# Six of 64 chunk stores issued by GpSimd in pieces of seven and eight rows

## The chip, the cores and the metric

The kernel runs on one core of a Trainium2 chip. The core has five engines that this text names: PE (TensorE, matrix products), DVE (VectorE), ACT (ScalarE), POOL (GpSimd) and SP (SyncE, which here issues loads only). Sixteen DMA engines move data between the chip's memory (HBM) and the core's on-chip memory SBUF, whose 128 rows are called partitions; PE writes into a second on-chip memory, PSUM. DMAs are issued by SP, ACT or GpSimd, each through a queue of its own. The metric is device time in microseconds (us) for one execution; lower is better.

## What is computed

The input is an image of 512 by 512 pixels with 192 channels, in bfloat16. The channels fall into four groups of 48, and each group is multiplied with its own 48 by 48 matrix (a grouped convolution with a window of one pixel):

```python
H = W = 512; G = 4; C = 192; Cg = 48; k = 1
x: (1, H, W, C) bfloat16        w: (1, 1, G, Cg, Cg) bfloat16

xg = x.reshape(1, H, W, G, Cg)
out = einsum('bhwgc,gcd->bhwgd', xg, w[0, 0])
return out.reshape(1, H, W, C)
```

So 262,144 pixels come in and go out, 384 B each: 100.66 MB in and as much out.

## The kernel before

**Tiling.** The pixels are cut into 64 chunks of 4096 pixels. A chunk is a tile of 128 partitions by 32 pixels, so that a partition's row is 32 x 384 = 12,288 B without a break in HBM, and a chunk is 1536 KB. rows_view (L102) gives a chunk's rows of the input or output. There are NB = 5 input buffers x_sb and 5 output buffers o_sb; chunk n uses buffer n mod 5 of each.

**Work on a chunk.** A chunk is eight groups of four pixels a partition. For each group PE makes six transposes (L192) of 128 by 128 from x_sb into PSUM (xT_ps); DVE copies the result to SBUF (L242, xT_sb); PE multiplies the six pieces with a prepared weight tile wt (L214, into o_ps in PSUM); and the result goes from o_ps to o_sb as bfloat16. That last step, the eviction, is ACT's (L285, both halves of a group), but in three groups of ten (SHARE, L34) ACT takes one half (L282) and DVE the other (L249). PE transposes two groups ahead of the products (LOOK).

**Order and waits.** Each engine runs its own list of instructions, and semaphores hold it back. The Waiter class (L37) leaves out a wait that an earlier one already covers.

- SP issues the load of chunk n (L160) once PE has transposed all of chunk n - 5.
- ACT issues the store of chunk n in its function store (L255 to L269), when it has come to the third group of the next chunk: the wait on mm_done (L263) is for the product two groups after the chunk's last, by which its evictions are known to be done.
- A store is one DMA of 128 rows. It adds 16 to the semaphore st_sem of its buffer, one for each DMA engine that has written its part. Before ACT writes the first group of chunk n into o_sb, it waits for the store of chunk n - 5 (L274); DVE does the same (L246). The amounts to wait for are counted by store_parts and st_total (L106 to L112).
- GpSimd makes two constants at the start (L140 to L151, the identity for the transposes and a selection tile for the weights) and does nothing afterwards.
- At the end ACT waits for all stores (L291).

The names RELIEF and RELIEF_ROWS (L28, L29) let chosen stores be issued in several ranges of rows; RELIEF is empty, so no store is split. The lines that issue a store:

```python
dst = rows_view(of, n)
for (r0, r1) in store_parts(n):
    act.dma_start(dst[r0:r1, :], o_sb[b][r0:r1, 0:sizes[n] * C]).then_inc(st_sem[b], 16)
```

Of the kernel before, what the change touches and what calls it, by code (L numbers as in the profile page):

```python
# [6 lines left out]
BF16 = mybir.dt.bfloat16  # L7
# [4 lines left out]
C = GROUPS * CG  # L12
# [12 lines left out]
PPC = 32  # L25
NB = 5
TAIL = (32, 32, 32, 32)
RELIEF = ()  # L28
RELIEF_ROWS = ((0, 128),)  # L29
NXP = 4  # L30
NOB = 4
NXS = 4
# [17 lines left out]
def shared(g):  # L50
    return (g % 10) in SHARE


def bass_standalone__grouped__vision_kernel(nc, x, w, out):
# [9 lines left out]
    sizes = [PPC] * n_mid + list(TAIL)  # L64
    n_chunks = len(sizes)

    xf = x.rearrange("b h w c -> (b h w) c")
    of = out.rearrange("b h w c -> (b h w) c")
# [12 lines left out]
    g1 = [g0[n] + sizes[n] // 4 for n in range(n_chunks)]  # L81
# [14 lines left out]
    def actT_cnt(g):  # L96
        return g - GT + 1

    def dveT_cnt(g):
        return sum(1 for h in range(GT, g + 1) if shared(h))  # L100

    def rows_view(ap, n):  # L102
        s = sizes[n]
        return ap[pix0[n]:pix0[n] + 128 * s, :].rearrange("(p i) c -> p (i c)", p=128)

    def store_parts(n):  # L106
        return RELIEF_ROWS if n in RELIEF else ((0, 128),)

    st_total, acc = [], [0] * NB
    for n in range(n_chunks):  # L110
        acc[n % NB] += 16 * len(store_parts(n))
        st_total.append(acc[n % NB])  # L112

    def st_before(n):
        return st_total[n - NB] if n >= NB else 0

    with ExitStack() as es:
        block = es.enter_context(nc.Block())
        x_sb = [es.enter_context(nc.sbuf_tensor(f"x_sb{i}", [128, PPC * C], BF16)) for i in range(NB)]
        o_sb = [es.enter_context(nc.sbuf_tensor(f"o_sb{i}", [128, PPC * C], BF16)) for i in range(NB)]  # L120
# [2 lines left out]
        esel = es.enter_context(nc.sbuf_tensor("esel", [CG, ECOLS], BF16))  # L123
        w_sb = es.enter_context(nc.sbuf_tensor("w_sb", [CG, GROUPS, CG], BF16))
        wt = es.enter_context(nc.sbuf_tensor("wt", [128, WCOLS], BF16))
        xT_ps = es.enter_context(nc.psum_tensor("xT_ps", [128, NXP, 1024], BF16))
        o_ps = es.enter_context(nc.psum_tensor("o_ps", [128, NOB, 512], F32))

        def sem(name):
            return es.enter_context(nc.semaphore(name))  # L130

        ld_sem = [sem(f"ld{i}") for i in range(NB)]
        st_sem = [sem(f"st{i}") for i in range(NB)]
        w_sem, id_sem, e_sem, wb_sem = sem("w_sem"), sem("id_sem"), sem("e_sem"), sem("wb_sem")
        p0_sem, p1_sem, wc_sem = sem("p0_sem"), sem("p1_sem"), sem("wc_sem")
        t_done, mm_done = sem("t_done"), sem("mm_done")
        ev1_sem, ev2_sem, act_sem = sem("ev1_sem"), sem("ev2_sem"), sem("act_sem")
        ev2T_sem, actT_sem = sem("ev2T_sem"), sem("actT_sem")

        @block.gpsimd  # L140
        def _(gp):
            gp.memset(esel[:], 1.0).then_inc(p0_sem, 1)  # L142
            gp.memset(ident[:], 1.0).then_inc(p1_sem, 1)  # L143
            gp.wait_ge(p0_sem, 1)
            gp.affine_select(out=esel[:], in_=esel[:], pattern=[[-1, ECOLS]],  # L145
                             compare_op=AluOpType.is_equal, fill=0.0, base=ESHIFT,
                             channel_multiplier=1).then_inc(e_sem, 1)
            gp.wait_ge(p1_sem, 1)
            gp.affine_select(out=ident[:], in_=ident[:], pattern=[[-1, 128]],  # L149
                             compare_op=AluOpType.is_equal, fill=0.0, base=0,  # L150
                             channel_multiplier=1).then_inc(id_sem, 1)  # L151

        @block.sync
        def _(sp):
# [77 lines left out]
        @block.vector  # L232
        def _(dve):
            wq = Waiter(dve)
            wq.wait(wb_sem, 1)
            dve.tensor_copy(wt[:], o_ps[:, NOB - 1, 0:WCOLS]).then_inc(wc_sem, 1)  # L236
            waited_chunk = -1
            for (op, g) in dve_prog:
                n, lg = groups[g]
                if op == "ev1":  # L240
                    wq.wait(t_done, g + 1)
                    dve.tensor_copy(xT_sb[g % NXS][:], xT_ps[:, g % NXP, 0:2 * UC]).then_inc(ev1_sem, 1)  # L242
                else:
                    if waited_chunk != n:
                        waited_chunk = n
                        wq.wait(st_sem[n % NB], st_before(n))  # L246
                    wq.wait(mm_done, g + 1)
                    u = lg * 2 + 1
                    dve.tensor_copy(o_sb[n % NB][:, u * UC:(u + 1) * UC],  # L249
                                    o_ps[:, (2 * g + 1) % NOB, 0:UC]).then_inc(  # L250
                                        ev2_sem if g < GT else ev2T_sem, 1)

        @block.scalar
        def _(act):
            wq = Waiter(act)  # L255
            act.sem_inc(act_sem, 2)
            pending = []

            def store(n):
                b = n % NB  # L260
                g = g1[n] - 1
                if g < GT:
                    wq.wait(mm_done, g + 3)  # L263
                else:
                    wq.wait(actT_sem, actT_cnt(g))
                    wq.wait(ev2T_sem, dveT_cnt(g))
                dst = rows_view(of, n)
                for (r0, r1) in store_parts(n):
                    act.dma_start(dst[r0:r1, :], o_sb[b][r0:r1, 0:sizes[n] * C]).then_inc(st_sem[b], 16)  # L269

            for g in range(NG):
                n, lg = groups[g]
                if lg == 0:
                    wq.wait(st_sem[n % NB], st_before(n))  # L274
                wq.wait(mm_done, g + 1)
                while pending and pending[0][1] <= g:
                    store(pending.pop(0)[0])
                v = (2 * g) % NOB
                ob = o_sb[n % NB]
                if shared(g):  # L280
                    u = lg * 2
                    ins = act.copy(ob[:, u * UC:(u + 1) * UC], o_ps[:, v, 0:UC])  # L282
                else:
                    dst = ob[:, lg * 2 * UC:(lg + 1) * 2 * UC].rearrange("p (u c) -> p u c", u=2)
                    ins = act.copy(dst, o_ps[:, v:v + 2, 0:UC])  # L285
                ins.then_inc(act_sem if g < GT else actT_sem, 1)
                if g == g1[n] - 1:
                    pending.append((n, g + 2 if g < GT else g + 1))
            for (n, _) in pending:
                store(n)  # L290
            for b in range(NB):  # L291
                act.wait_ge(st_sem[b], acc[b])
# [28 lines left out]
```

## Time and profile before

| | |
|---|---|
| device time, median of 3 runs | 494.31 us (494.1 to 494.51) |
| the profiled execution | 494.62 us, of which the span from the first to the last instruction is 492.9 us |
| granted clock of TensorE, mean over the span | 0.986 |
| busy, share of the span | PE 84%, DVE 71%, ACT 71%, POOL 0% |
| HBM read, written | 100.68 MB, 100.66 MB; 409 GB/s together, mean over the span |
| loads | 64 of 1536 KB on SP's queue (q1), median 30.9 us from issue to landing |
| stores | 64 of 1536 KB on ACT's queue (q10), median 30.5 us from issue to landing |

How to read the profile: the page cuts the span into 40 equal slices; each digit is the busy share of a slice in tenths, 9 standing for 90% and more. DMA is the mean busy share of the 16 DMA engines. The chain of waits follows the work that ended last back from the end: at each step to what released it. A group of instructions is given by line, engine, operation, written and read tile, count, busy time, mean duration of one, and the idle time before it. ACTq and SPq are the instructions by which an engine issues DMAs. "Issue to landing" is the time from that instruction to the last of the DMA's semaphore increments.

### The profile page before, as it was taken

Reading aid. Unit: us, or ns where it says so; the run is one execution under the profiler, and the core shown is the slowest. Engines: PE = TensorE matmul, PEld = TensorE weight load, DVE = VectorE, ACT = ScalarE, POOL = GpSimd, SP = SyncE. Lnnn points to the kernel's source line nnn. Section 1 sums busy time; section 2 is a strip of 40 time slices with the busy share of each in tenths; the row PEclk is TensorE's granted clock in tenths of the full one; section 3 lists DMA queues with packets and bytes.
Section 4 is the critical chain, followed back from the end, with each engine's and each line's share of the span. In section 5 each row is a group of like instructions: output and inputs, shape, how many; then the busy total and the mean of one; then the engine's idle time right before and its main releaser. Section 6 shows DMA issues by size and latency. Waiting matters only on the chain.

```text
span 492.9 us, 15013 instructions
## 1 busy us (share of the span) xinstructions
PE 415.4 (84%) x6154; PEld 390.5 (79%) x6154; DVE 348.0 (71%) x666; ACT 349.0 (71%) x513; POOL 1.3 (0%) x8
## 2 busy tenths in 40 slices
PE   4888999999999888888888888888888888888880
PEld 4788999999989887787777877878778787787770
DVE  2767888888888776776776767677667767777760
ACT  1757888888888767677677776766767667676680
POOL 1000000000000000000000000000000000000000
PEclk9989999999999999999999999999999999999995
DMA  8999999999999999999999999999999999999563
GB/s 342 398 428 426 427 429 427 428 428 428 429 428 429 430 429 430 429 430 428 427 430 430 429 429 429 430 428 427 429 428 430 428 427 430 430 430 430 213 266 144
DMA packets 18658, 201.56 MB, mean 409 GB/s; under 512 B 2256, under 2 KB 2256, under 8 KB 2256
## 3 DMA queue, kind: packets, MB, share of 16 engines
q1 hardware_dynamic: 9424, 100.69, 48.3%
q10 hardware_dynamic: 9216, 100.67, 48.2%
q8 instruction: 7, 0.11, 0.1%
q14 instruction: 11, 0.09, 0.0%
HBM read 100.68 MB, written 100.66 MB: 409 GB/s over the span
## 4 chain that ended last, share of the span: by engine, by line
DMA 67%; PE 2%; ACT 1%; ACTq 0%; issue 0%
DMA out_dram<-o_sb 67%; PE o_ps L214 1%; ACT o_sb L285 1%; PE xT_ps L192 1%; ACTq L269 0%; ACT o_sb L282 0%; ACTq L47 0%
## 5 line engine op out<-in xcount | busy, mean ns | idle before, releaser
L285 ACT CAST o_sb<-o_ps 128x768 bf16<-128x768 f32 x359 | 280.1, 799 | 99.9 <-PE o_ps L214 65.4
L242 DVE COPY xT_sb<-xT_ps 128x768 bf16<-128x768 bf16 x512 | 282.3, 554 | 89.4 <-PE xT_ps L192 84.3
L214 PE MATMUL o_ps<-wt,xT_sb 128*128 128x144 bf16 (+1 forms) x3072 | 297.5, 233 | 46.9 <-PEq L169 40.5
L192 PE MATMUL xT_ps<-ident,x_sb 128*128 128x128 bf16 x3072 | 256.7, 220 | 10.0 <-PEq L169 4.9
L214 PEld LDWEIGHTS o_ps<-wt,xT_sb 128*128 128x128 bf16 x3072 | 210.9, 98 | 64.4 <-issue 51.5
L192 PEld LDWEIGHTS xT_ps<-ident,x_sb 128*128 128x128 bf16 x3072 | 196.8, 98 | 17.2 <-issue 17.1
L249 DVE CAST o_sb<-o_ps 128x384 bf16<-128x384 f32 x153 | 84.6, 553 | 32.9 <-DMA out_dram<-o_sb 20.0
L282 ACT CAST o_sb<-o_ps 128x384 bf16<-128x384 f32 x153 | 73.4, 480 | 30.7 <-DMA out_dram<-o_sb 19.6
L178 PE MATMUL o_ps<-w_sb,esel 48*128 48x48 bf16 x10 | 0.6, 209 | 7.3 <-DMA w_sb<-in_w_dram 7.3
L236 DVE CAST wt<-o_ps 128x480 bf16<-128x480 f32 x1 | 0.7, 658 | 7.9 <-PE o_ps L178 7.9
L178 PEld LDWEIGHTS o_ps<-w_sb,esel 48*128 48x128 bf16 x10 | 0.5, 110 | 7.3 <-issue 7.3
L285 ACT ACT_TABLE_LOAD x1 | 1.3, 1283 | 0.9 <-PEq L306 0.9
L145 POOL TENSOR_SCALAR_AFFINE_SELECT esel<-esel 48x272 bf16<-48x272 bf16 x1 | 0.4, 406 | 0.0
L142 POOL MEMSET esel<- 48x272 bf16 x1 | 0.3, 318 | 0.3 <-POOLq L306 0.3
L149 POOL TENSOR_SCALAR_AFFINE_SELECT ident<-ident 128x128 bf16<-128x128 bf16 x1 | 0.3, 286 | 0.0
L143 POOL MEMSET ident<- 128x128 bf16 x1 | 0.2, 198 | 0.0
L306 POOL MEMSET const-bfloat16-1.0<- 128x1 bf16 x1 | 0.1, 102 | 0.0
L306 POOL MEMSET const-uint8-127<- 128x1 uint8 x1 | 0.1, 102 | 0.0
L306 POOL MEMSET const-float32-1.0<- 128x1 f32 x1 | 0.1, 99 | 0.0
L306 POOL MEMSET const-float32-0.0<- 128x1 f32 x1 | 0.1, 98 | 0.3 <-issue 0.3
## 6 DMA issues: line engine op xcount, KB each, us to landing
x_sb<-in_x_dram SPq DMA_DIRECT2D x64, 1536.0 KB, 30.9
out_dram<-o_sb ACTq DMA_DIRECT2D x64, 1536.0 KB, 30.5
w_sb<-in_w_dram SPq DMA_DIRECT2D x1, 18.0 KB, 5.9
```

Source lines behind the costliest of these rows:

```text
L142: gp.memset(esel[:], 1.0).then_inc(p0_sem, 1)
L145: gp.affine_select(out=esel[:], in_=esel[:], pattern=[[-1, ECOLS]], compare_op=AluOpType.is_equal, fill=0.0, base=ESHIFT, channel_multipli ...
L149: gp.affine_select(out=ident[:], in_=ident[:], pattern=[[-1, 128]], compare_op=AluOpType.is_equal, fill=0.0, base=0, channel_multiplier=1) ...
L178: last = pe.matmul(o_ps[:, NOB - 1, col:col + CG], lhsT=esel[:, s0:s0 + 128], rhs=w_sb[:, g, :], start=True, stop=True, skip_group_check=True)
L192: last = pe.transpose(xT_ps[:, g % NXP, j * 128:(j + 1) * 128], x_sb[b][:, col:col + 128], ident[:])
L214: last = pe.matmul(o_ps[:, v, c0:c1], lhsT=xs[:, j * 128:(j + 1) * 128], rhs=wt[:, WOFF[tc]:WOFF[tc] + (c1 - c0)], start=(tc == 0), stop=( ...
L236: dve.tensor_copy(wt[:], o_ps[:, NOB - 1, 0:WCOLS]).then_inc(wc_sem, 1)
L242: dve.tensor_copy(xT_sb[g % NXS][:], xT_ps[:, g % NXP, 0:2 * UC]).then_inc(ev1_sem, 1)
L249: dve.tensor_copy(o_sb[n % NB][:, u * UC:(u + 1) * UC], o_ps[:, (2 * g + 1) % NOB, 0:UC]).then_inc(ev2_sem if g < GT else ev2T_sem, 1)
L282: ins = act.copy(ob[:, u * UC:(u + 1) * UC], o_ps[:, v, 0:UC])
L285: ins = act.copy(dst, o_ps[:, v:v + 2, 0:UC])
L306: nc = _bacc.Bacc("TRN2", target_bir_lowering=False, num_devices=1)
```

## The change

Stores 5, 14, 23, 32, 41 and 50 (RELIEF) are no longer one DMA on ACT's queue. GpSimd issues them, in pieces, once the same product count is reached on which ACT's store waits.

- For each of eight values j a piece of seven rows is stored (rows r, r + 4, ... r + 24, where r runs over 0 to 3 and 32 to 35), then a "skip" follows, then a piece of eight rows (64 + r, ... in steps of four).
- A skip copies one element in each of so many partitions of a small new tile, scratch, to another column of it. It is a DMA like the others and stores nothing of the result..
- The pieces leave out rows 28 to 31 and 60 to 63 (QUADS). quad_home gives each such group of four one of three ways: ACT stores it as a DMA of four rows (act_parts), or GpSimd does, with a skip of 12 behind it, or with a skip of 4 ahead and one of 8 behind. Over the six stores each way is taken by four of the twelve groups.

In sum GpSimd issues 164 DMAs (104 of rows and 60 skips) and ACT 58 whole stores and four of four rows. ACT and DVE get one more wait each ahead of chunk n: for the pieces of chunk n - 5, on the new semaphores gs_sem. GpSimd waits for its own DMAs at the end. The other 58 stores, the loads and all computation are as before.

```diff
-RELIEF = ()
-RELIEF_ROWS = ((0, 128),)
+RELIEF = tuple(range(5, 55, 9))
+QUADS = (28, 60)
+
+
+def quad_home(n, q):
+    return (2 * RELIEF.index(n) + q) % 3
+
+
+def act_parts(n):
+    if n not in RELIEF:
+        return [(0, 128)]
+    return [(QUADS[q], 4) for q in range(2) if quad_home(n, q) == 0]
+
+
+def gp_parts(n):
+    parts = []
+    for j in range(8):
+        r = 32 * (j // 4) + j % 4
+        parts += [("rows", r, 4, 7), ("skip", 1)]
+        if j in (3, 7):
+            home = quad_home(n, j // 4)
+            if home == 1:
+                parts += [("rows", QUADS[j // 4], 1, 4), ("skip", 12)]
+            elif home == 2:
+                parts += [("skip", 4), ("rows", QUADS[j // 4], 1, 4), ("skip", 8)]
+        parts.append(("rows", 64 + r, 4, 8))
+    return parts
...
-        acc[n % NB] += 16 * len(store_parts(n))
+        acc[n % NB] += 16 * len(act_parts(n))
...
+    def gs_total(b, n):
+        return 16 * sum(1 for m in RELIEF if m % NB == b and m <= n
+                        for part in gp_parts(m) if part[0] == "rows")
...
+        scratch = es.enter_context(nc.sbuf_tensor("scratch", [16, 160], BF16))
...
+        gs_sem = [sem(f"gs{i}") for i in range(NB)]
+        sc_sem, cur_sem = sem("sc_sem"), sem("cur_sem")
...
+            gp.memset(scratch[:], 0.0).then_inc(sc_sem, 1)
+            gp.wait_ge(sc_sem, 1)
+            wq = Waiter(gp)
+            nd = 0
+            for n in RELIEF:
+                b = n % NB
+                wq.wait(mm_done, g1[n] + 2)
+                dst = rows_view(of, n)
+                for part in gp_parts(n):
+                    if part[0] == "rows":
+                        _, r, step, c = part
+                        r_end = r + step * (c - 1) + 1
+                        gp.dma_start(dst[r:r_end:step, :], o_sb[b][r:r_end:step, :]).then_inc(gs_sem[b], 16)
+                    else:
+                        nd += 1
+                        gp.dma_start(scratch[0:part[1], 2 * nd:2 * nd + 1],
+                                     scratch[0:part[1], 0:1]).then_inc(cur_sem, 16)
+            gp.wait_ge(cur_sem, 16 * nd)
+            for b in range(NB):
+                wq.wait(gs_sem[b], gs_total(b, n_chunks))
...
                         wq.wait(st_sem[n % NB], st_before(n))
+                        wq.wait(gs_sem[n % NB], gs_total(n % NB, n - NB))
...
-                for (r0, r1) in store_parts(n):
-                    act.dma_start(dst[r0:r1, :], o_sb[b][r0:r1, 0:sizes[n] * C]).then_inc(st_sem[b], 16)
+                for (r, c) in act_parts(n):
+                    act.dma_start(dst[r:r + c, :], o_sb[b][r:r + c, :]).then_inc(st_sem[b], 16)
...
                 if lg == 0:
                     wq.wait(st_sem[n % NB], st_before(n))
+                    wq.wait(gs_sem[n % NB], gs_total(n % NB, n - NB))
```

## The prediction

> **What bounds the kernel now.** I read the page's slices first, then the chain of waits, then the stretches at the end, then the times at which single DMAs land.
>
> ```profile
> PE   4888999999999888888888888888888888888880
> DMA  8999999999999999999999999999999999999563
> GB/s 342 398 428 426 427 429 427 428 428 428 429 428 429 430 429 430 429 430 428 427 430 430 429 429 429 430 428 427 429 428 430 428 427 430 430 430 430 213 266 144
> DMA 67%; PE 2%; ACT 1%; ACTq 0%; issue 0%
> ```
>
> No compute engine is full; the 16 DMA engines are, up to the last three slices, where the rate falls to a half and less. The chain is made of stores.
>
> ```profile
> 376.12 30.56 DMA out_dram<-o_sb
> 406.68 0.02 issue
> 406.70 0.01 ACT o_sb L282
> 406.71 30.53 DMA out_dram<-o_sb
> ```
>
> One link is a store of 30.5 us; its landing frees a buffer, ACT runs on, issues another store (L269), and that one sets the next link, four chunks later: 30.5/4 = 7.64 us a chunk. The stretches of the end (first the stretch, then the engines, then clock, DMA share, GB/s) tell whose 7.64 us that is:
>
> ```profile
> 400.00:452.00 52.00, 44.61 (x668) 41.73 (x666) 37.34 (x73) 36.91 (x55) 0.00 (x0) 1.00 1.01 428
> 452.00:460.00 8.00, 6.76 (x104) 6.23 (x101) 5.93 (x12) 5.22 (x8) 0.00 (x0) 1.00 0.77 325
> 460.00:486.00 26.00, 16.48 (x246) 15.41 (x246) 13.56 (x26) 16.41 (x24) 0.00 (x0) 0.94 0.61 255
> 486.00:492.00 6.00, 0.00 (x0) 0.00 (x0) 0.00 (x0) 0.00 (x0) 0.00 (x0) 0.50 0.06 25
> ```
>
> From 486 us a share of 0.06 is left: one engine of sixteen, at 25 GB/s. The trace also records the 16 increments of each store's semaphore, one per DMA engine (us after the span's start):
>
> ```
> store   first   15th    last
>   16   148.18  150.64  154.21
>   36   294.49  297.80  307.26
>   56   440.79  444.71  460.16
>   59   457.48  461.16  477.60
>   63   485.34  485.53  492.32
> ```
>
> From store 16 to 56 the first comes every (440.79 - 148.18)/40 = 7.315 us, the last every 7.649. A chunk is 8 rows of 12,288 B in and 8 out on each engine (128 rows over 16), so 0.457 us a row on the early engines and 0.478 on one. One DMA engine is 4.6% slower, every chunk waits for it, and behind it fifteen engines have nothing to do at the end: (0.23 x 8 + 0.39 x 26 + 0.94 x 6) x 16/15 = 18.8 us each. The four last stores land 3.64 us apart on it: with one queue left, it too takes 0.456 a row.
>
> **The change, part by part.** Stores 5, 14, ... 50 lose 8 of their 128 rows each on one engine (rows 28 to 31 and 60 to 63, if those are the late engine's).
> *Removed there:* 6 x 8 = 48 rows x 0.478 = 22.9 us. It would end at 492.32 - 22.9 = 469.4. The packet records have 12 ns for a 96 B packet and 9 ns for a completion; the 56 scratch packets that the pieces put there cost 0.7 us: 470.1. Its lag, 0.334 x 9 = 3.0 us from one such store to the next, goes back by 3.8 each time, so in between it holds nobody up.
> *Added to the others:* 48 rows in 12 groups of four, spread by quad_home over three sets of four engines: 4 rows each on twelve of them, 4 x 0.457 = 1.83 us, nothing on three. Their own 48 rows of these stores stay theirs, in another queue.
> *What ends last then:* the fifteen. At store 59 they stand between 457.48 and 461.16 and have four stores of 3.64 left, 14.6 us, without a break. With 1.83 of added rows and 0.55 from the last landing to the span's end (492.87 - 492.32) the earliest is through at 474.5, the latest at 478.2. The profiled execution took 494.62 us, 1.72 more than its span (494.31 is the median of the runs): 476.2 to 479.9.
> *Completions:* the six stores become 164 GpSimd DMAs (six times 24, four homes of two, four of three). If each writes a completion on all 16 engines, that is 164 x 9 ns = 1.5 us each; it may overlap with data as those of today do: 0 to 1.5.
> *Tail:* after the last load (the fifteen have it at 455.7) chunk 63 still needs eight groups of some 0.75 us (the timeline's spacing of PE) and its issue, 7 us; meanwhile four stores, 14.6 us, are in the queues. That covers it.
> *Issue on GpSimd.* POOL is idle after 2 us, and the trace has no DMA of its own. A store becomes 24 + 20/6 = 27.3 DMAs in a row, behind one wait on mm_done; nothing else is queued on POOL. The buffer is wanted again four chunks later, 4 x 7.315 = 29.3 us. So with about 2 us for the last piece to land (three queues share an engine, 3 x 0.457, and on the late engine 0.45 passes today from the last row's end at 491.87 to its landing) an issue may take (29.3 - 2)/27.3 = 1.0 us before ACT's and DVE's new wait on gs_sem is felt. Behind that wait stand all evictions of chunk n+5 and, on ACT, store n+4, and PE waits for both; the loads stay ahead by five buffers. The price of an issue: below, the shortest instruction of POOL, 0.10 us; above, the whole way of the smallest DMA, issue to landing, 5.9 us.
>
> ```profile
> w_sb<-in_w_dram SPq DMA_DIRECT2D x1, 18.0 KB, 5.9
> L306 POOL MEMSET const-float32-0.0<- 128x1 f32 x1 | 0.1, 98 | 0.3 <-issue 0.3
> 452.59 0.34 ACTq L269 DMA_DIRECT2D out_dram<-o_sb  x1
> ```
>
> The nearest row is the same operation on ACT's queue, 0.34 us for 128 rows; I take 0.34, so 9.3 us a store, hidden in the 29.3. Without that cover each further 0.1 us costs 2.7 us a store. [...]
> *ACT* loses six issues of 0.34 and keeps four, of four rows. ACT is busy 71%: nothing.
> *Sum:* 494.62 - 22.9 on the late engine uncovers the fifteen, 476.2 to 479.9, and 0 to 1.5. The end is that of the latest one, but part of its lag is single jumps of about 1 us, and three engines get no row more. I take **478.5 us**.
>
> **Rivals.**
> *GpSimd's issue becomes the bound (slower).* From one such store to the next run 27.3 issues, 2 us, then chunks n+5 to n+9 and two groups at PE's pace (42 x 0.75 = 31.5 us); nine chunks at the DMA pace are 65.8. So the point is (65.8 - 33.5)/27.3 = 1.18 us an issue, and past it 164 issues pay in full: at 1.5 us 478.5 + 0.32 x 164 = 531, at 2 us 613. For it: the trace has no issue of POOL, whose shortest and longest instruction (0.10 and 0.41 us) bound nothing of this kind, and 27 in a row add up. Against: 1.18 is 3.5 times the nearest row.
> *The relieved engine isn't the late one, or the cursor doesn't move as supposed.* The profile doesn't number its engines, so nothing in it says that the rows left out are the late one's. Then the late engine keeps 1024 rows, and gets up to 4 more (1.9 us): 494.3 to 496.5. If every piece starts at the same engine, the first seven or eight get 48 rows more: 461.16 + 14.6 + 52 x 0.457 = 499.5, and 502 with what lies behind it. [...]
> *The pieces are dearer on the engines.* The records of the run's first packets have 0.94 to 1.14 us for a row instead of 0.46. If each of the 48 to 52 rows that come by GpSimd's queue pays a third of that excess, 0.2 us, the fifteen end 10 us later: 489. For it: each piece brings an engine one row only, as if its queue began anew. Against: those first packets met idle engines, and here two other queues keep an engine at work (share 1.01 where two run).
>
> **How the numbers follow.** The forecast has 0.56, in its own range of 473 to 483 (below: the earliest engine without an added row, 476.2 - 1.8, and one jump of lag less; above: the latest with all completions, 481.4, and two jumps more); dearer pieces 0.08 (483 to 492), the wrong engine 0.18 (494 to 502), GpSimd's issue 0.18 (above 495, mostly above 502). The range of 473 to 502 takes in all but GpSimd's issue, so that about 2 in 10 are left out. A difference of 0.2%, 1 us, is about what this kernel's runs can tell from none (494.1 to 494.51). Faster: 0.56 + 0.08 = 0.64; same: 0.03 out of the wrong-engine case; slower: 0.15 + 0.18 = 0.33.
>
> **What would show it.** The last increments of the stores come every 7.3 us and within 5 us of the first; the stretch of 0.06 DMA share at the end is gone, and the rate stays at 428 to within 15 us of the end. GpSimd's DMAs are under 1 us from one to the next, and the 24 to 29 of one store under 29 us. No ACT or DVE wait on out_dram grows past 2 us. The forecast is wrong if one engine still ends 10 us behind (wrong engine), if several do (cursor), or if ACT and DVE wait 10 us or more, six times (issue).

## The result and the profile after

The changed kernel takes 559.48 us in the median of four runs (557.22 to 560.76), the kernel before 494.39: 1.131 times as long, 95% interval 1.127 to 1.135. The prediction was 478.5 us with a range of 473 to 502; it was wrong in size and in sign.

The page of the kernel after, its slices first, then its DMA queues, the chain, and the groups of GpSimd's DMAs:

```profile
PE   4989970899941999914999809999339999059995
DMA  8999996799994899975999958999948999759985
GB/s 348 406 429 425 428 423 251 289 384 428 404 408 186 338 407 425 418 324 190 390 426 421 426 220 334 389 428 416 377 197 331 428 424 407 300 217 392 428 343 226
...
q10 hardware_dynamic: 8384, 91.43, 38.7%
q0 software_dynamic: 5248, 9.26, 4.7%
...
PE 3%; ACT 2%; ACTq 0%; issue 0%
...
L193 POOL DMA_DIRECT2D out_dram<-o_sb x104 | 53.8, 521 | 377.9 <-PE o_ps L263 377.9
...
out_dram<-o_sb POOLq DMA_DIRECT2D x48, 96.0 KB, 16.2
```

Six times the rate falls to half, and PE stands still with it (the zeros and ones of its row); before, the rate held at 428 until the end. GpSimd issues a piece in 0.52 us, but the piece lands 16 us after its issue in the median. The 164 DMAs of the new queue, q0, appear as 5248 packets, 32 for each, though they carry only 752 rows (104 pieces of four, seven or eight). The waits of the same kernel (engine, line, what for: us in total, times, the longest) say who stood still, and the stretches around the first such store what the DMA engines did:

```profile
ACT o_sb L336 <- DMA out_dram<-o_sb: 74.2, 4, 20.0
DVE o_sb L299 <- DMA out_dram<-o_sb: 54.4, 3, 19.5
ACT o_sb L333 <- DMA out_dram<-o_sb: 38.7, 2, 19.6
```

```profile
54.00:60.00 6.00, 5.66 (x88) 5.35 (x86) 4.68 (x10) 4.84 (x8) 4.94 (x10) 1.00 1.01 427
60.00:83.00 23.00, 20.43 (x312) 19.46 (x309) 17.89 (x34) 16.82 (x25) 8.49 (x17) 1.00 1.01 426
83.00:97.00 14.00, 0.00 (x0) 0.00 (x0) 0.00 (x0) 0.00 (x0) 0.00 (x0) 0.56 0.65 274
97.00:100.00 3.00, 0.28 (x3) 0.30 (x4) 0.00 (x0) 1.22 (x2) 0.00 (x0) 0.50 0.17 70
```

```profile
55.06 0.67 POOL L193 DMA_DIRECT2D out_dram<-o_sb  x1 [52.93 <-PE o_ps L263]
67.97 0.52 POOL L193 DMA_DIRECT2D out_dram<-o_sb  x1
98.78 0.80 ACT L336 CAST o_sb<-o_ps 128x768 bf16<-128x768 f32 x1 [18.79 <-DMA out_dram<-o_sb]
```

GpSimd begins at 55.06 us and has issued its 26 DMAs by 68.5; their last packet runs at 97.8. ACT waits from 80 to 98.8 for the buffer, all compute engines are empty from 83 to 97, and the DMA engines, which have only what is queued, run dry. Over the six stores the last packet comes 41.5 to 44.4 us after the first issue, where the buffer is wanted after 29.3. Between 64 and 84 us the queues stand like this (packets, MB, share):

```profile
q1 hardware_dynamic: 368, 4.04, 47.5%
q10 hardware_dynamic: 347, 3.87, 45.5%
q0 software_dynamic: 369, 0.64, 8.5%
```

Three queues get nearly the same number of packets, whatever their size: 369 packets, most of them of 4 B, against 368 and 347, most of them rows of 12,288 B. That is the reading from which the main theory comes: the queues get turns, a packet each, whatever its size. The packet records show the other half of it. The 164 GpSimd DMAs have 5248 packets and 2624 increments of their semaphores, 32 and 16 to a DMA; 752 packets are rows, 144 are elements of skips (2 B) and 4352 have 4 B. Before, ACT's 64 stores had 1024 packets of 4 B, one for each increment; taken in the same way, 2624 of the 4352 are completions, and 1728 are fillers. Spread evenly, that is two packets of a DMA on each of the 16 engines: a row, an element of a skip or a filler, and a completion. The even spread is an assumption, since the records don't number the engines.

### The profile page after: what moved, and what is told of

Read it like the earlier page. It is cut to its first block, busy times and chain, and to the rows that moved or that the text cites. A ratio compares the mean times of both kernels' runs of the same rounds, so it can differ in the third digit from the quotient of the medians.

```text
span 558.7 us, 15181 instructions
## 1 busy us (share of the span) xinstructions
PE 419.6 (75%) x6154; PEld 401.4 (72%) x6154; DVE 348.2 (62%) x666; ACT 349.6 (63%) x513; POOL 85.4 (15%) x173
## 3 DMA queue, kind: packets, MB, share of 16 engines
q0 software_dynamic: 5248, 9.26, 4.7%
## 5 line engine op out<-in xcount | busy, mean ns | idle before, releaser
L263 PE MATMUL o_ps<-wt,xT_sb 128*128 128x144 bf16 (+1 forms) x3072 | 304.0, 236 | 123.9 <-PEq L218 120.3
L263 PEld LDWEIGHTS o_ps<-wt,xT_sb 128*128 128x128 bf16 x3072 | 215.1, 99 | 141.4 <-issue 131.0
L241 PE MATMUL xT_ps<-ident,x_sb 128*128 128x128 bf16 x3072 | 261.9, 223 | 1.0 <-issue 1.0
L241 PEld LDWEIGHTS xT_ps<-ident,x_sb 128*128 128x128 bf16 x3072 | 202.9, 100 | 1.5 <-issue 1.2
L193 POOL DMA_DIRECT2D out_dram<-o_sb x104 | 53.8, 521 | 377.9 <-PE o_ps L263 377.9
L196 POOL DMA_DIRECT2D scratch<-scratch x60 | 31.1, 519 | 0.0
## 6 DMA issues: line engine op xcount, KB each, us to landing
out_dram<-o_sb POOLq DMA_DIRECT2D x48, 96.0 KB, 16.2
```

The costliest lines, as they stand in the source:

```text
L193: gp.dma_start(dst[r:r_end:step, :], o_sb[b][r:r_end:step, :]).then_inc(gs_sem[b], 16)
L196: gp.dma_start(scratch[0:part[1], 2 * nd:2 * nd + 1], scratch[0:part[1], 0:1]).then_inc(cur_sem, 16)
L241: last = pe.transpose(xT_ps[:, g % NXP, j * 128:(j + 1) * 128], x_sb[b][:, col:col + 128], ident[:])
L263: last = pe.matmul(o_ps[:, v, c0:c1], lhsT=xs[:, j * 128:(j + 1) * 128], rhs=wt[:, WOFF[tc]:WOFF[tc] + (c1 - c0)], start=(tc == 0), stop=( ...
```

## The experiments

**Theory (turns).** On an engine with two other full queues each packet of GpSimd's queue waits for a row of both, 2 x 0.457 = 0.914 us, so 1.83 us a DMA; 27.3 of them and the rows themselves take longer than the buffer may be away. **Rivals:** the rows that go by the third queue are slow in themselves (rows theory); a GpSimd DMA takes a fixed time one after the other, whatever the other queues carry (round-trip theory). All ratios are to the kernel before on the same chip.

### 1. The scratch DMAs left out

```diff
-        parts += [("rows", r, 4, 7), ("skip", 1)]
+        parts += [("rows", r, 4, 7)]
-                parts += [("rows", QUADS[j // 4], 1, 4), ("skip", 12)]
+                parts += [("rows", QUADS[j // 4], 1, 4)]
```

> The 60 scratch DMAs are left out; the 104 row DMAs stay, 17.3 a store instead of 27.3. Turns theory (each GpSimd DMA puts two packets on each of the 16 engines, and each of them waits for one row of both other queues, 2 x 0.457 us, so 1.83 us a DMA): the last piece of a store lands about 17.3 x 1.83 = 32 us after the first issue instead of 43, the waits of ACT and DVE on these stores fall from 19 us each to 0 to 6, and the time lies between 494 and 515 us. Rows theory (the 120 rows of a store that go by the third queue are what is slow): the rows are the same, so 43 us, waits near 19 us, and 555 us or more.

Measured 538.11 us (1.093, 1.090 to 1.097). The last packet comes 38 to 41 us after the first issue, and ACT waits 16 us each time. This lies between both expectations and decides nothing: the forecast had left out some 4 us from the first issue to the first packet (4.2 to 4.5 here) and the rows' own time, 8 x 0.457 = 3.7 us if they are dealt evenly. With both, 34.7 x 0.914 + 7.7 = 39.4, as measured, but found afterwards, and no proof: the same sum gives 57.7 for the change, where 41.5 to 44.4 were measured. There the other two queues run dry in the stall, and the turns come faster (GpSimd's queue has 369 packets in the 20 us from 64 to 84 us, beside 715 of the other two, and 138 in the 4 us from 88 to 92, beside 86); experiment 7, in which they don't, is the test of this sum.

### 2. Each of the six stores as one GpSimd DMA

```diff
 def gp_parts(n):
...
+    return [("rows", 0, 1, 128)]
```

> The six stores are one GpSimd DMA of 128 rows each, no scratch DMAs. Turns theory: 8 rows and one or two small packets an engine, 10 turns of at most 1.37 us: landed within 14 us, no wait on them, and as no engine is relieved about 494 us (492 to 496). Rows theory: the same rows through the third queue, so some 40 us a store and 550 us.

Measured 495.06 us (1.006, 1.004 to 1.009), no wait on these stores, and this row in the list of issues:

```profile
out_dram<-o_sb POOLq DMA_DIRECT2D x6, 1536.0 KB, 15.5
```

The same rows through the same queue land in 15.5 us instead of 43. The rows theory falls. Compared with experiment 1, a store of 16 DMAs fewer has its last packet 23 to 26 us sooner.

### 3. One DMA of 120 rows, and few small ones

```diff
+    parts = [("rows", 0, 1, 120), ("skip", 1)]
+    if RELIEF.index(n) % 3 < 2:
+        parts += [("rows", 120, 1, 8), ("skip", 8)]
+    return parts
```

> A relieved store is one GpSimd DMA of 120 rows, one scratch DMA of one row, and the last 8 rows as one GpSimd DMA and a scratch DMA of 8 (four stores) or as two ACT DMAs of four (two stores); one scratch DMA of 8 rows at the start. So at most 4 GpSimd DMAs a store. Turns theory: 8 + 1 rows and 7 small packets, 16 turns of at most 1.37 us, landed within 22 us, no waits of 10 us and more. If the one engine that gets no row of the 120 is the late one, the time is what the prediction gave, 476 to 482 us; if it is another (or the rows are dealt otherwise) 494 to 499 us. Rows theory: above 540 us.

Measured 502.46 us (1.020, 1.014 to 1.026). GpSimd issues the 120 rows and one or three more DMAs; in two stores the last eight rows go by ACT in fours. The only wait on a store is one of 0.8 us, as the turns theory expects, but there is no gain; the time is over the 494 to 499 us of the second case. After the first such store one engine lands its part of load 14 at 91.6 us, 3.8 ahead of the next at 95.4 (8 x 0.457 = 3.7): the engine left out. It runs ahead from then on, and another is still last. The left-out engine isn't the late one. The packet records have these rows at 0.61 us in the mean instead of 0.46; what makes them dearer was not tried.

### 4. 120 and 8 rows on ACT's queue

```diff
+    return [(0, 120), (120, 8)]
```

> Nothing by GpSimd: the six stores go by ACT's queue as 120 rows and 8 rows. This asks which engine is late. If the 120 rows leave out the late engine, it saves 48 rows of 0.478 us, and the others get up to 6 rows of 0.457 more: 477 to 483 us. If the engine left out is another, the late one keeps its rows and may get 6 more: 494 to 498 us. No theory of the third queue says anything of this kernel but that it has no waits of 10 us and more.

Measured 500.77 us (1.015, 1.011 to 1.019), somewhat over the second case. At load 62 one engine is still 10.3 us behind the fifteenth (465.26 against 454.98), so the 120 rows left out another engine, and the late one kept its rows. Six rows more on the late engine would be 2.9 of its 8.4 us; where the rest comes from was not tried.

### 5 and 6. Smaller packets in the other two queues, with the change and without

```diff
-                sp.dma_start(x_sb[b][:, 0:sizes[n] * C], rows_view(xf, n)).then_inc(ld_sem[b], 16)
+                for i in range(4):
+                    w0, w1 = 1536 * i, 1536 * (i + 1)
+                    sp.dma_start(x_sb[b][:, w0:w1], rows_view(xf, n)[:, w0:w1]).then_inc(ld_sem[b], 16)
```

ACT's stores are cut into halves in the same way.

> The changed kernel with each load cut into four column quarters (3,072 B a packet) and each ACT store into two halves (6,144 B): same bytes, smaller packets in the two other queues; GpSimd's pieces are as they were. Turns theory: a turn of GpSimd's queue now waits for 0.114 + 0.228 = 0.342 us of other work instead of 0.914, so 54.7 turns cost 19 us, with 8 rows of 0.457 and 4 us from the issue to the first packet about 26 us instead of 43: the waits of ACT and DVE on these stores shrink from 19 us to under 3, and the time falls below 500 us (476 to 485 if the relieved engine is the late one). Round-trip theory (each GpSimd DMA costs some 1.55 us whatever the other queues carry): 43 us as before, waits near 19 us, about 559 us.

> The kernel before with the same cut of loads and stores, for comparison: both theories expect 494 us give or take 5, since bytes and the late engine stay; what it differs by is the price of the cut itself.

With the change 538.91 us (1.093, 1.089 to 1.096), without it 513.03 (1.039, 1.035 to 1.043). The cut alone costs 20 us, which neither theory had. The point in question is clear all the same: the last packet of the six stores comes 24 to 28.5 us after the first issue (26 forecast, 43 in the change), ACT and DVE have no wait on a store at all, and the pieces land as follows, against 16.2 us in the change:

```profile
out_dram<-o_sb POOLq DMA_DIRECT2D x48, 96.0 KB, 5.7
```

GpSimd's DMAs were untouched and became faster because the rows of the other queues became shorter. The round-trip theory falls. But 538.9 is 26 us above 513.0: a second loss remains when the stalls are gone.

### 7 and 8. Nine output buffers, with the change and without

```diff
+NBO = 9
...
-                        wq.wait(gs_sem[n % NB], gs_total(n % NB, n - NB))
+                        wq.wait(gs_sem[n % NBO], gs_total(n % NBO, n - NBO))
```

All uses of o_sb, st_sem and gs_sem count to nine.

> The changed kernel with nine output buffers instead of five; GpSimd's pieces and all packets as in the change. A relieved store may now take eight chunks, 58 us, before ACT and DVE want its buffer. Both theories of why it takes 43 us (turns: up to 58 with the other queues kept full) expect no waits of 10 us and more: the stalls go, and what the change does to the DMA engines themselves is seen alone: 476 to 483 us if the relieved engine is the late one, 494 to 502 if not. If the loss of the change were not in the buffers but in what the pieces cost the DMA engines, it stays near 559 us.

> The kernel before with nine output buffers, for comparison. The late engine has its 1024 rows as before and was never without work: 492 to 495 us. If buffers alone were what held the kernel before, it falls below 485 us.

With the change 519.57 us (1.054, 1.050 to 1.058), without it 492.37 (0.999, 0.997 to 1.001). One wait on a store is left:

```profile
ACT o_sb L334 <- DMA out_dram<-o_sb: 3.7, 1, 3.7
```

The last packet now comes 51.5 to 60.2 us after a store's first issue, against 57.7 by the sum of full turns in experiment 1 (the fifth store is left out: there GpSimd itself issued nothing for 30.3 us after its 128th DMA, and why is open). So the turns are as long as the theory has them, and with nine buffers they hold hardly anybody up: the stalls cost 559.5 - 519.6 = 40 us. Buffers alone don't help, as the late engine is the bound. The remaining 27 us are about the 26 of experiments 5 and 6, found in another way. A single load's 16 landings show where they arise. Load 15, after the first piecewise store, lands in this kernel at (us)

```
97.2 97.6 97.9 98.1 99.8 100.6 100.6 101.0 101.2 | 106.0 106.0 107.7 108.5 109.5 109.9 111.1
```

Nine engines are ahead and seven some 9 us behind. Neither expectation has this. The last part of load 63 lands at 503.3 us here and at 470.4 in experiment 8: one engine is far later than without the change.

### 9. Sixteen pieces of eight rows

```diff
+        parts += [("rows", r, 4, 8), ("rows", 64 + r, 4, 8)]
```

> Nine output buffers, and the six stores as 16 GpSimd pieces of eight rows each (rows r, r + 4, ... of the lower and of the upper half in turn), no scratch DMAs, nothing by ACT. It asks on which engines pieces of eight rows land. Cursor theory (each piece goes on where the last one ended): lower and upper pieces take turns on two sets of eight engines, each engine gets 8 rows a store, and the landings of a load spread by no more than the 3 to 5 us that they have anyway, but for the late engine. Fixed-start theory (each piece begins at the same engine): eight engines get 16 rows a store and eight none; after the first such store half of the landings of a load come some 16 x 0.457 = 7.3 us ahead of the other half, after the second twice that, up to the depth of the buffers; the time is above 505 us.

Measured 519.87 us (1.055, 1.051 to 1.060; two runs). Load 15 lands at

```
97.6 97.7 97.8 97.8 99.8 100.0 100.1 100.2 | 104.7 105.1 105.1 105.6 105.8 106.4 106.6 110.3
```

Eight and eight, some 7 us apart (16 x 0.457 = 7.3), and at load 22 the two groups are at 143.6 to 145.7 and 164.2 to 171.9. So these pieces begin at the same engine each time; there is no cursor that goes on. The late engine is among the eight with double rows: at load 60 fifteen engines land between 455.4 and 457.7 us and one at 481.8, 24 us behind; in experiment 8 the late engine is 13 us behind there (447.7 against 434.9). The nine and seven of experiment 7 fit the same reading: the change's pieces of seven rows on one set of seven engines, those of eight on the same seven and one more, so that seven engines get 16 rows a store instead of 8, one keeps 8 and the other eight get none (the groups of four come on top). The two queues also differ in their small packets: a piece of eight rows by GpSimd has 32 packets (3072 for the 96 here), while ACT's queue in experiment 4 has 9258, which are 8192 rows, 16 more for each of 58 whole stores and 138 for the six pairs of 120 and 8 rows, 15 and 8 a pair if it is one for each engine that gets rows.

### 10. As many DMAs, but each piece on all 16 engines

```diff
+        parts += [("rows", 16 * j, 1, 16)] + [("skip", 1)] * (2 if j < 5 else 3)
```

With nine output buffers.

> Nine output buffers, and each of the six stores as eight GpSimd pieces of 16 rows with 19 scratch DMAs of one row between them: 27 DMAs as in the change, but every engine gets one row of every piece. If the 27 us that the change still costs with nine buffers come from rows that are dealt unevenly over the engines: no such loss, 491 to 500 us. If they come from the number of GpSimd's DMAs and their turns: as with the change's pieces, 515 to 524 us.

Measured 509.47 us (1.033, 1.029 to 1.037): between the two. The packet records have these rows, 16 neighbours at a time, at 0.817 us in the mean; 6 x 8 of them at 0.36 above the usual are 17 us an engine, and 492.4 + 17 is what was measured. That sum was made after the run, and it can't be the whole account: experiment 17 has as many DMAs without dear rows and still loses 10 us.

### 11. Twenty-six scratch DMAs, then the whole store

```diff
+    return [("skip", 1)] * 26 + [("rows", 0, 1, 128)]
```

With five buffers.

> Five output buffers, and each of the six stores as 26 scratch DMAs of one row, then one GpSimd DMA of 128 rows. All engines get equal rows, no engine is relieved; only the 27 DMAs stand ahead of the buffer's release. Turns theory: 52 turns before the first row, then 8 rows a engine and more: landed after 40 to 55 us, ACT and DVE wait 15 to 25 us six times, and the time is 494 plus six stalls, 525 to 560 us. If the stalls of the change came from its rows or their dealing and not from the count of DMAs: waits under 5 us and about 495 us.

Measured 529.54 us (1.075, 1.072 to 1.078), and the waits are back:

```profile
ACT o_sb L326 <- DMA out_dram<-o_sb: 54.5, 4, 14.6
DVE o_sb L289 <- DMA out_dram<-o_sb: 39.2, 3, 13.4
ACT o_sb L323 <- DMA out_dram<-o_sb: 26.5, 2, 13.5
```

The scratch DMAs move one element each; 26 of them ahead of a store that alone lands in 15.5 us (experiment 2) delay it to 37 to 39 and cost 37 us in six stores. The count of DMAs is enough to stall the kernel, without their rows or their dealing. The waits are just under the 15 to 25 us of the forecast, because ACT's queue runs dry in the stall and the last turns come faster: from 87.5 to 91.5 us it has no packet, and GpSimd's has 282, against 435 in the 20 us from 58 to 78, when ACT's has 303.

### 12 to 16. Extra rows on the first engines

The kernel before with 24 small loads into spare buffers that nothing reads:

```diff
+                if n in EXTRA:
+                    i = EXTRA.index(n)
...
+                    sp.dma_start(spare[i % 4][0:4 * EROWS - 3:4, :],
+                                 rows_view(xf, n - 6)[0:4 * EROWS - 3:4, :]).then_inc(ex_sem[i % 4], 16)
```

EROWS is 7, 2, 4, 6 and 5.

> The kernel before with 24 small loads more on SP's queue, one every second chunk: seven rows of 12,288 B each (rows 0, 4, ... 24 of a chunk), into spare buffers that nothing reads. Each adds one row to seven engines. The fifteen have 18.8 us to spare. If the late engine is none of the seven: 24 x 0.457 = 11 us on engines that have it to spare, 491 to 495 us. If it is one of them, 24 x 0.478 = 11.5 us more: 502 to 506 us.

> As the kernel with 24 extra loads of seven rows, with two rows each (0 and 4), so that two engines get one row more from each. Late engine among these two: 502 to 508 us, as with seven. Late engine none of them: 491 to 495 us.

> The same with four rows each (0, 4, 8, 12). Late engine among the first four: 502 to 508 us. Not among them: 491 to 495 us.

> The same with six rows each (0 to 20 in steps of four). Late engine among the first six: 502 to 508 us. If it is the seventh: 491 to 495 us here and about 507 with seven rows. If the 15 us of the seven rows came from the extra loads as such and not from where their rows land, all three of these kernels lie near 505 us, or rise with the number of rows.

> As the kernels with 24 extra loads, with five rows each (0 to 16 in steps of four). With four rows 494.6 us were measured and with six 507.3. Late engine the fifth: about 507 us here; late engine the sixth: about 495.

```
rows a load   2        4        5        6        7
us            494.82   494.64   507.16   507.32   507.39
ratio         1.004    1.005    1.030    1.030    1.030
```

A step between four and five rows, and none elsewhere: if each load's rows go one to an engine in a fixed order, the fifth engine of that order is the late one. The runs were spread over three chips, so this takes the late engine to be the same one on each; on the chip of the five-row run, experiment 18 shows that it isn't among the first four of ACT's queue. The first four take 11 us more work for 2 us of time, the fifth makes its 11.5 into 15. The one step bears out a fixed order; on which engine the rows that the change spares in a whole store, 28 to 31 and 60 to 63, are dealt was not tried by itself.

### 17. The 27 DMAs with even rows and nine buffers

The edit of experiment 11 on nine buffers.

> Nine output buffers, and each of the six stores as 26 scratch DMAs of one row and one GpSimd DMA of 128 rows: 27 DMAs as in the change, rows dealt evenly and each row from its usual engine, no buffer wanted early. If the 17 us of the kernel with 16-row pieces came from its rows (0.82 us each instead of 0.46, and 6 x 8 of them on an engine make 17 us) and the 27 us of the change's pieces from uneven dealing, then nothing is left: 491 to 497 us. If the turns of 162 GpSimd DMAs cost the DMA engines time in themselves: 505 us or more.

Measured 502.33 us (1.020, 1.017 to 1.024): ten too many for the one case, three too few for the other. Waits of some 8 us on these stores are still there, so nine buffers didn't quite hold them:

```profile
ACT o_sb L324 <- DMA out_dram<-o_sb: 15.3, 2, 8.0
ACT o_sb L327 <- DMA out_dram<-o_sb: 13.5, 2, 8.3
```

Around the third to sixth store loads take 0.51 to 0.55 us a row in the packet records instead of 0.46 (190 to 210, 260 to 280, 330 to 345 and 395 to 420 us), but around the first, under 910 small packets between 60 and 105 us, they take 0.46. So the small packets alone don't make the rows dear. How the 10 us divide between waits and rows is open.

### 18. A try at a faster kernel

One store as 124 and 4 rows on ACT's queue, with nine buffers:

```diff
-RELIEF = ()
-RELIEF_ROWS = ((0, 128),)
+RELIEF = (30,)
+RELIEF_ROWS = ((0, 124), (124, 128))
```

> A try at a kernel better than before: nine output buffers, and store 30 alone cut by ACT into 124 rows (4 x 31) and 4 rows, so that, if the rows are dealt to as many engines as divide them, all of it lands on four engines that the extra rows showed not to be late; no DMA by GpSimd. The late engine loses 8 rows of 0.478 us, 3.8 us; the four get 24 rows of 0.457 more, 11 us of the 18.8 that they have to spare: 488 to 490 us against 492.4 for nine buffers alone. If the rows are dear there (0.8 us, as the 16-row pieces were), the four need 22 us and become the late ones: 494 to 498 us.

Measured 492.22 us (0.9995, 0.997 to 1.002): no gain. The rows of store 30 land at eight times from 271.0 to 277.8 us, read here as two for each of four engines. The counts of the changed kernel fit that: on ACT's queue 58 whole stores and four DMAs of four rows have 944 packets of 4 B, and with 16 for a whole store, as before, four are left for each of the small ones. The landings of other stores, the last five one by one, show what became of the late engine (us):

```
store  1st to 11th         12th    13th    14th    15th    last
  29   243.1 to 244.5     245.0   245.0   245.1   246.6   252.5
  31   250.4 to 252.4     260.1   279.2   280.4   283.9   285.1
  63   483.6 to 483.7     483.8   484.4   486.4   489.7   490.1
```

The late engine goes on from 252.5 to 260.1 us, one step of 7.6 for two stores: it was relieved of store 30, and it is through at 483.8 us, against 489.8 in experiment 8. But the four engines that took its rows, 24 more on each, are now the last, up to 490.1 us. By the landings of experiment 8 the latest of the fifteen is at 461.5 us at store 59 and has four stores of 3.64 left, so it had 13.7 us to spare before 489.8 and not 18.8; 24 x 0.457 is 11, and ACT's rows were dearer for a while (0.487 us in the mean from 260 to 280 us). The gain was taken by the engines that got the rows; spreading them over more engines was not tried. Load 60 (last part 447.1 us, 447.7 in experiment 8) doesn't show the relief; only a store's rows were moved. No version was found that beats the kernel before.

## Why the prediction was wrong

**The bound before: right.** One late engine sets the pace, with 0.478 us a row where the others have 0.457. Experiment 8 (more buffers, no gain) and the extra rows (11 us free on four engines, 15 us lost on the fifth) bear it out.

**The step that failed first: "with about 2 us for the last piece to land (three queues share an engine, 3 x 0.457 ...)".** It counted one turn for the whole store. With 32 packets spread evenly over 16 engines each of the 27.3 DMAs takes two turns on an engine, fillers and completions too, so the queue needs 55 turns, not one. In place of 2 us behind the last issue the runs showed 28 to 30 us behind it (last issue 13 to 15 us, last packet 41 to 44 us after the first). The sentence on completions, "164 x 9 ns = 1.5 us", was the same mistake in another place: it took the 9 ns that such a packet lasts for its price, while its price in its queue was the wait for its turn, 0.914 us by the theory (27.3 DMAs of 1.83 us and 7.7 us: 57.7 us a store, 51.5 to 60.2 measured in experiment 7). Experiments 5, 7 and 11 show this part by itself; the stalls are worth 40 us of the 65. What the turns cost besides stalls is not separated (experiment 17).

**The issue: size off, without effect.** 0.52 us against 0.34 assumed, 14 us a store, far below the 1.0 us at which it would have been felt. The 164 issues took 0.52 to 0.67 us each, with VectorE 62% busy. From a store's first issue to its first packet 4.0 to 4.3 us passed in the changed kernel, for which the forecast has no term of its own.

**The rival that came true in its effect.** "GpSimd's issue becomes the bound" had the place of the loss, the wait on gs_sem, and the point from which it decides, 1.18 us a DMA. Measured from the first issue to the last packet it is 1.51 to 1.64 us a DMA, and its price, 478.5 + (1.58 - 1.18) x 164 = 544 us, is nearer than the forecast. But its mechanism is refuted, so this nearness is luck: GpSimd was done after 13 to 15 us. It is the DMA engines' turns.

**"Removed there: 6 x 8 = 48 rows x 0.478 = 22.9 us": the sign was wrong.** This rested on two suppositions of the prediction: that each GpSimd DMA's rows go on at the engine where the last DMA's ended (the cursor), and that rows 28 to 31 and 60 to 63 are the late engine's. No run shows either, and none shows 22.9 us taken off. What the runs showed in their place are pieces that begin at the same engine each time (experiment 9) and a late engine that is the fifth in the order of the extra loads' rows (12 to 16) and, with pieces of eight rows, among the eight with double rows (24 us behind at load 60 in experiment 9). With the change's pieces it would belong to those that get 16 rows of each of these stores, 48 more than before; 48 x 0.478 = 22.9 us added to 492.4 is 515, against 519.6 measured with the stalls gone. So the 27 us are probably for the most part the gain with the sign turned. This is an argument from the landings, and a rival stands beside it: with the changed pieces a load's row takes 0.486 us in the mean, with the kernel before on nine buffers 0.464, and over the 512 load rows of an engine that is 11 us. How much of this falls on the late engine the records, which don't number the engines, can't tell. A kernel that puts rows on the late engine alone was not made; experiment 18 took 8 rows off it, and its end came 6 us earlier.

**"Their own 48 rows of these stores stay theirs"** failed with it: by the reading of the landings (nine engines ahead and seven some 9 us behind in experiment 7, eight and eight in experiment 9) eight engines had none, seven double, one its own number. No run shows the 1.83 us of the sum either, four added rows on each of twelve engines. **The rival of the wrong engine** was thus true as well, and its 502 for pieces that start at one engine was too low because it left the late engine at 1024 rows.

**Sum:** of the 65 us, 40 are stalls by turns, through five buffers, and the rest is what nine buffers leave (27 us on the chip of experiment 7), by the argument above mostly dealing. Both are differences between measured kernels, so that they add up is no test of the account.

## What to carry to other kernels

In a kernel like this one, where three queues share the DMA engines, price a small DMA by its turns: the number of its packets on an engine, fillers and completions included, times a packet of every other full queue. Here a packet of 4 B took a turn as a row of 12,288 B did (369 packets against 368 and 347 in 20 us), and this sum gave 57.7 us a store where 51.5 to 60.2 were measured. Before rows are moved off a slow engine, find out by extra rows which engine is slow and by the landings of one later load where the pieces really fall; both are cheap runs, and a profile that doesn't number its engines leaves both open. Before rows are given to other engines, find out how many each can take: in experiment 18 four engines took 24 each and became the last. A price that the profile doesn't have deserves a bound for each place at which it can arise, the queue behind the issue as well as the issue.

## What was not expected of the hardware

- A GpSimd DMA of at most 16 rows or elements has 32 packets and 16 increments, however little it carries: in the change 164 DMAs have 5248 packets and 2624 increments, in experiment 1 the 104 pieces have 3328 packets, in experiment 10 162 DMAs have 5184.
- After its 128th DMA GpSimd issued nothing for 30.3 us in experiment 7 and 32.6 us in experiment 10, but not in the change. Why is open.
- Cutting loads to 3,072 B and stores to 6,144 B a packet slowed the kernel before from 492.7 to 513.0 us, though no byte was added.
- Rows moved 16 neighbours at a time took 0.82 us each instead of 0.46 (experiment 10).
- The late engine is late only in company: before, it took 0.478 us a row while two queues ran and 0.456 with one, at the end. Why it is late was not asked.
